# Packed half blocks in the second stage of a two-stage attention kernel, and two exponentials taken out of ScalarE's set order

## Chip, cores and metric

The kernel runs on one core of a Trainium2 chip. The metric is the device time of one execution in microseconds: the median of several runs. The profile is of one execution; its page's "span" goes from the first to the last instruction.

## What is computed

There are two stages. The first is attention with soft-capped scores over 8 batches, 12 heads, 448 positions, 64 per head. The second is a layer of four attention experts on its output (768 wide), causal, of which each position uses the two with the largest gate.

```python
# first stage
scores = scale * np.matmul(q, k.transpose(0, 1, 3, 2))
scores = cap * np.tanh(scores / cap)
attn = np.exp(scores - max); attn = attn / attn.sum(-1)
x = attn @ v                                   # then [batch, 448, 12 * 64]
# second stage
logits = x @ w_gate                            # 4 experts, the top 2 of each position kept
for e in range(4):
    q, k, v = x @ wq[e], x @ wk[e], x @ wv[e]  # 64 wide
    a = softmax(causal(scale * q @ k.T))
    ye = a @ v @ wo[e]
    out += (weight of e where e is chosen) * ye
```

## The kernel before

**First stage.** The 96 heads go in 48 pairs p (six pairs, `HP`, to a batch). A pair's scores are filled by TensorE into PSUM in three parts: "X" (two banks for a first chunk of 128 keys, a third for the last 64 keys of both heads), "Y1" and "Y2" (two banks each, one tile Y for both, so that Y2 can only be filled once ScalarE has read Y1). ScalarE takes the tanh of each part (`tanh`, L907) and then the exponential of a whole pair in one instruction (`expo`, L919). These instructions have a set order, `fixed=True`: X and Y1 of pair p, the exponential of pair p - 1, Y2 of pair p. The fills are `fill` and `heads` (L854) and `tails` (L864); the score matmuls of two heads sum over 64 rows each and sit in the two halves of TensorE's rows. The product with V is `pv` (L934, L942), its division `xk` on VectorE, its transposes `xt`. The pairs of the last batch (42 to 47) leave out their last queries, which come as two more units, 48 and 49 (`NPV` = 50).

**Second stage.** Batch b's work runs under the first stage's pairs of batch b + 1: V, gate and K and Q projections (`b_v`, `b_gate`, `b_qk`), then for each of two slots s (a position's first and second choice) a masked query qm, scores (`b_score`), one exponential, the causal masks (`causal`), the product with V (`b_pv`), then the sum of both slots (`b_ot`, on GpSimd, "POOL") and the output projection (`b_wo`). Since qm is zero where an expert isn't chosen, the four experts' scores are one matmul over 256 rows, done as two of 128 (r = 0, 1). From batch 4 on (`MD`) the mask is transposed by a DMA (mT). The scores of a slot are laid out in 1024 columns of two banks: three diagonal blocks of 128 by 128, and the rest below the diagonal, with two blocks of 64 columns at either end for the last 64 positions (`H0`, `H1`). The exponential (L1301) of the 1024 columns belongs to the set order: `exps` says after which pair's Y1 it stands; a pair in `alone` has its X fill apart from the fill of Y2 of the pair before. The mask is two selects on GpSimd (L1311, L1318). The product reads blocks of 128 by 128 from `cols(n)`: 1, 2, 3 and 4 matmuls of 260 columns for the four query blocks n.

**Batch 7** has no pairs after it: `last`, `last2` and `normed` do its second stage at the end, with its own layout (`eL` exponentials at L1577, masks at L1585) in the tiles pP of the other batches.

**Order of the work.** Every operation is entered in a graph with an engine, a planned duration (`occ`), what it reads and writes, and a due time. `dues` derives due times backwards from the set order of ScalarE (`when`); `solve` plays a list schedule and fixes the order in which each engine gets its instructions. `RANKS` holds, from a planned time on, offsets in hundredths of a microsecond to the due times of single operations. Engines run their queues in order; SyncE ("SP") issues most DMAs. PSUM banks are taken from `AUX` (three A banks), `XB` and `YB` by `Group`. The chip's waits follow from the tiles touched, not from the planned times; a row entered in the graph's write list only keeps the order.

Of the kernel before, what the change touches and what calls it, by code (L numbers as in the profile page):

```python
# [25 lines left out]
    (7.5, {  # L26
        136: 93, 174: 305, 290: -418,
    }),
    (27.5, {
        507: 475,  # L30
    }),
    (67.5, {
        678: -572, 692: 231, 735: -81, 738: -31, 741: 513, 841: 473, 1112: 748, 1167: -284,
    }),
    (87.5, {
        716: 497, 727: -643, 760: -112, 767: -1037, 862: 1282, 888: 375, 919: 264,
    }),
    (127.5, {
        1092: 467, 1196: 214, 1239: -453, 1249: 345, 1267: 323, 1277: 281, 1398: -60, 1401: 289,
        1405: 243, 1449: -132, 1535: 337, 1537: 820,  # L40
    }),
    (147.5, {
        1338: 97, 1345: 117, 1355: 477, 1387: -702, 1413: 186, 1525: 119, 1548: -196,
    }),
    (167.5, {
        1600: 205, 1607: 294,
    }),
# [7 lines left out]
    }),  # L55
    (254.5, {
        2520: -331, 2577: -265, 2635: -902, 2645: 2133, 2659: 128, 2667: 486, 2678: 522, 2702:
        -188, 2703: -340, 2706: -238, 2713: -937, 2729: -581, 2766: 2204, 2788: 297,
# [3 lines left out]
TURN = 2.2  # L62
SAIL = 1.1
SHIP = 1.25
# [10 lines left out]
MD = 4  # L75
# [23 lines left out]
class Graph:  # L99
# [232 lines left out]
def kernel(  # L332
# [26 lines left out]
    W1 = 320  # L359
# [90 lines left out]
    def turned(n, dst, src, r, w, name, due=None):  # L450
# [35 lines left out]
    pP = [sb(f"pP{i}", [128, 2, 64 + 1024]) for i in range(2)]  # L486
# [17 lines left out]
    vL = sb("vL", [128, E, Dh + 1])  # L504
    p2 = yp[NPV % NYP].rearrange("p a s -> p (a s)")[:, 0 : E * 512].rearrange(
        "p (e c t) -> p e c t", e=E, c=4)
    oTL = [sb(f"oTL{i}", [128, 2, 128]) for i in range(3)]
# [107 lines left out]
    def setup_b():  # L615
# [20 lines left out]

        def pz():
            for t in pB:
                nc.gpsimd.memset(t[:, 0:64], 0.0)

        gp(0.6, pz, w=[("pB", i) for i in range(4)])
# [110 lines left out]
    def tr(p):  # L752
# [45 lines left out]
        if p >= KD:  # L798
            pe(0, lambda: tq(g, 0, 2), [("q16", i), "ident"], [("tps", p, "q")], g, occ=0.1,
               name=f"trq{p}")  # L800
            pe(0, lambda: tq(g, 2, 4), [("q16", i), "ident"], [("tps", p, "r")], g, occ=0.1)
            def qe():
# [7 lines left out]
                [("qk", t, "q"), ("qkw", t)], g, name=f"qk{p}")  # L810
# [85 lines left out]
    alone = {0, 1, *exps}  # L896
# [228 lines left out]
    def b_v(b, ref):  # L1125
        x = b % 2
        j1 = PJ if b == LB - 1 else 0
        for n in range(4):
            g = Group(AUX + XB, 1.8)
            hr = [("half", "v", n)] if b == LB - 1 else []  # L1130
            for j0 in range(j1, NDC, 2):
# [14 lines left out]
                [("vps", b, n)] + hr, [("vB", x, n)], g, name=f"vB{b}")  # L1146

    def b_qk(b, ref):
        x = b % 2
        for r in range(2):  # L1150
            for which in "kq":
# [4 lines left out]
                for j in range(j1, NDC):  # L1156
# [4 lines left out]
                       [(which, b, r)], g, name=f"{which}{b}_{r}",  # L1161
# [81 lines left out]
    def b_mask(b, s):  # L1243
# [9 lines left out]
        if b < MD:  # L1253
            for r in range(2):
# [8 lines left out]
                pe(0, mm, [("mB", s), "ident"], [("mt", b, s, r)], g, occ=0.22, name=f"mT{b}")  # L1263
# [14 lines left out]
    def keys(c):  # L1278
        o = S - 128 if c == KC else 128 * c
        return slice(o, o + 128)  # L1280

    def b_score(b, s):
        x = b % 2
        for part, bk in ((H1, "X1"), (H0, "X0")):
            for i, (o, c, q0, n) in enumerate(part):
                def mm(o=o, c=c, q0=q0, n=n):
                    ps = BANK[f"X{o // 512}"]
                    a = min(n, max(KM - q0, 0))
                    for d, m, t in ((0, a, q0 + TL), (a, n - a, max(q0 - KM, 0))):
                        for r in range(2):  # L1290
                            if m:
                                nc.tensor.matmul(  # L1292
                                    ps[:, o % 512 + d : o % 512 + d + m], kB[x][r][:, keys(c)],
                                    qm[s][r][:, t : t + m], start=(r == 0), stop=(r == 1),
                                )

                pe(0, mm, [("kB", x, r) for r in range(2)] + [("qm", s, r) for r in range(2)],
                   [("s", bk)], occ=2 * c_pe(n), name=f"sB{b}_{s}", takes=(bk,) if i == 0 else ())
        pi = 2 * (b % 2) + s
        pb = pB[pi]  # L1300
        act(c_act(1024), lambda: nc.scalar.activation(  # L1301
            pb[:, 64:], PART["X"].rearrange("p a c -> p (a c)"), AF.Exp, scale=isc),
            [("s", "X0"), ("s", "X1")], [("pB", pi)], fixed=True, name=f"eB{b}_{s}",
            frees=("X0", "X1"))
        b_score.last = fixed_last()
        causal(pb, pi, "")

    def causal(pb, pi, nm):
        def diag():
            blk = pb[:, 128:512].rearrange("p (a c) -> p a c", a=3)  # L1310
            nc.gpsimd.affine_select(  # L1311
                out=blk, in_=blk, compare_op=ALU.is_ge, fill=0.0, base=0,
# [546 lines left out]
```

## Time and profile before

| | us |
|---|---|
| median of 3 runs | 305.21 (304.68 to 305.82) |
| the profiled execution | 304.79 |
| its span | 303.1 |
| ScalarE busy | 290.2 |
| TensorE busy (modelled ends) | 282.0 |
| VectorE busy | 213.5 |
| GpSimd busy | 189.4 |

The profiled execution's own time is 1.69 us longer than its span. A group of instructions in the profile reads: line, engine, operation, what is written and read, shapes, count, then busy time, mean ns of one, and the idle time of the engine just before. A row of a timeline reads: start, duration, then the instruction, with the idle time before it in brackets. A duration on ScalarE or TensorE overlaps the next instruction's, so that the cost of one is read from start to start.

### The profile page before, as it was taken

Reading aid. Unit: us, or ns where it says so; the run is one execution under the profiler, and the core shown is the slowest. Engines: PE = TensorE matmul, PEld = TensorE weight load, DVE = VectorE, ACT = ScalarE, POOL = GpSimd, SP = SyncE. Lnnn points to the kernel's source line nnn. Section 1 sums busy time; section 2 is a strip of 40 time slices with the busy share of each in tenths; the row PEclk is TensorE's granted clock in tenths of the full one; section 3 lists DMA queues with packets and bytes.
Section 4 is the critical chain, followed back from the end, with each engine's and each line's share of the span. In section 5 each row is a group of like instructions: output and inputs, shape, how many; then the busy total and the mean of one; then the engine's idle time right before and its main releaser. Section 6 shows DMA issues by size and latency. Waiting matters only on the chain.

```text
span 303.1 us, 8955 instructions
## 1 busy us (share of the span) xinstructions
PE 282.0 (93%) x3470; PEld 188.1 (62%) x3470; DVE 213.5 (70%) x630; ACT 290.2 (96%) x244; POOL 189.4 (62%) x537
## 2 busy tenths in 40 slices
PE   7897989999999999999999999999898999989992
PEld 4463546666666676667666676656665675657771
DVE  3354556866867877687887887697766878486972
ACT  5999999999999999999999999999999999989981
POOL 6793435997699664958799355927469305711580
PEclk9999999999999999999999999999999999999999
DMA  6999999999993399677996874455028751743136
GB/s 168 223 206 238 236 233 298 284 225 281 264 233 88 118 257 244 161 216 194 280 197 170 235 244 123 55 151 146 2 52 123 216 92 21 103 142 93 37 151 215
DMA packets 86874, 53.12 MB, mean 175 GB/s; under 512 B 47536, under 2 KB 83120, under 8 KB 86832
## 3 DMA queue, kind: packets, MB, share of 16 engines
q1 hardware_dynamic: 86448, 52.13, 69.8%
q8 instruction: 27, 0.44, 0.6%
q10 hardware_dynamic: 384, 0.43, 0.5%
q14 instruction: 15, 0.12, 0.2%
HBM read 36.19 MB, written 11.01 MB: 156 GB/s over the span
## 4 chain that ended last, share of the span: by engine, by line
ACT 64%; PE 15%; POOL 5%; DMA 5%; DVE 5%; issue 4%; ACTq 0%; DVEq 0%; POOLq 0%
ACT yp L907 33%; ACT yp L919 28%; ACT pP L1301 3%; DMA mT<-mB 3%; PE A L1413 2%; PE X L1292 2%; PE A L1088 2%; PE Y L854 1%; DMA ktf<-in_k_dram 1%; PE A L942 1%; POOL oS L1376 1%; POOL mB L1248 1%; PE A L1479 1%; DMA oT<-oS 1%; PE A L1514 1%
## 5 line engine op out<-in xcount | busy, mean ns | idle before, releaser
L919 ACT ACTIVATE yp<-yp 128x3136 f16<-128x3136 f16 (+4 forms) x51 | 142.4, 2794 | 0.0
L907 ACT ACTIVATE yp<-Y 128x896 f16<-128x896 f32 (+2 forms) x100 | 101.7, 1017 | 1.3 <-PE Y L854 1.3
L907 ACT ACTIVATE yp<-X 128x1344 f16<-128x1344 f32 (+2 forms) x50 | 68.3, 1367 | 0.4 <-PE X L854 0.3
L942 PE MATMUL A<-v,yp 128*128 128x65 f16 x1008 | 49.8, 193 | 0.0
L942 PEld LDWEIGHTS <-yp 128*128 128x128 f16 x1008 | 43.6, 97 | 4.0 <-issue 2.1
L934 PE MATMUL A<-vtz,yp 128*128 128x130 f16 x168 | 37.3, 222 | 3.9 <-ACT yp L919 1.6
L744 POOL CAST v<-vf 128x384 f16<-128x384 f32 x48 | 24.6, 519 | 20.8 <-PE A L942 13.1
L968 DVE TENSOR_TENSOR xk<-A,rca 128x256 f16<-128x256 f32 x84 | 35.3, 421 | 2.2
L708 POOL CAST q<-qf 112x512 f16<-112x512 f32 x44 | 26.6, 618 | 13.7 <-PE A L758 9.0
L439 DVE COPY ob<-A 128x384 f32<-128x384 f32 (+1 forms) x50 | 25.6, 550 | 2.4 <-PE A L1413 2.0
L817 DVE COPY qk<-A 128x960 f16<-128x960 f16 x32 | 20.3, 652 | 9.2 <-PE A L758 9.0
L934 PEld LDWEIGHTS <-yp 128*128 128x128 f16 x168 | 16.2, 97 | 16.1 <-issue 8.8
L854 PE MATMUL Y<-qk 64*128 64x448 f16 x136 | 24.7, 357 | 1.5 <-ACT yp L907 0.9
L1366 DVE SCALAR_TENSOR_TENSOR oB<-A,rcb,mw 128x256 f16<-128x256 f32 x55 | 25.3, 477 | 1.0
L1311 POOL TENSOR_SCALAR_AFFINE_SELECT pP<-pP 128x384 f16<-128x384 f16 x14 | 7.4, 528 | 29.3 <-ACT pP L1301 29.3
L965 DVE RECIPROCAL rca<-A 128x4 f32<-128x4 f32 x84 | 15.0, 178 | 14.2 <-PE A L942 13.2
L1413 PE MATMUL A<-wo,oT 128*128 128x384 f16 x106 | 22.8, 326 | 1.0 <-DVE qm L1170 1.0
L1351 PE MATMUL A<-vB,pP 128*128 128x260 f16 x138 | 22.2, 274 | 1.3 <-DVE oB L1366 0.5
L1028 DVE COPY xT<-A 128x448 f16<-128x448 f16 (+1 forms) x38 | 14.7, 386 | 11.2 <-PE A L1019 10.8
L1088 PE MATMUL A<-wvg,xT 128*128 128x260 f16 x168 | 21.3, 274 | 0.6 <-DVE oB L1366 0.3
L1376 POOL TENSOR_TENSOR oS<-oB,oB 128x512 f16<-128x512 f16 x14 | 16.1, 1155 | 8.2 <-issue 5.0
L758 PE MATMUL A<-ident,q 112*128 112x112 f16 x192 | 19.8, 214 | 0.7 <-DVE oB L1366 0.4
(240 smaller groups left out, 620.2 us busy)
## 6 DMA issues: line engine op xcount, KB each, us to landing
qf<-in_q_dram SPq DMA_DIRECT2D x23, 448.0 KB, 5.7
kf<-in_k_dram SPq DMA_DIRECT2D x23, 384.0 KB, 5.0
vf<-in_v_dram SPq DMA_DIRECT2D x23, 384.0 KB, 4.7
out_dram<-ob SPq DMA_DIRECT2D x21, 384.0 KB, 3.1
ktf<-in_k_dram SPq DMA_DIRECT2D x46, 32.0 KB, 5.0
vtf<-in_v_dram SPq DMA_DIRECT2D x46, 32.0 KB, 4.3
out_dram<-ob SPq DMA_DIRECT2D x6, 192.0 KB, 2.9
ob<-in_moe_wv_dram SPq DMA_DIRECT2D x2, 384.0 KB, 4.8
```

The source lines that it names most:

```text
L439: (nc.scalar.copy if o.eng == "ACT" else nc.vector.tensor_copy)(dst(), src())
L708: e(q16[i], qf[s][:, h].rearrange("p h (c d) -> p c h d", c=QC))
L744: nc.gpsimd.tensor_copy(v16[u][:, :, :, 0:Dh], vf[s][:, h].rearrange("p h (c d) -> p h c d", c=KC))
L854: nc.tensor.matmul(dst[:, g, o], kT[r, 128 * (c + 1) : 128 * (c + 2)], t[r, qs], start=True, stop=True,)
L907: ACTS[what, p] = act(c_act(n * (b - a)), lambda: nc.scalar.activation(y[:, a:b, 0:n], src[:, 0 : b - a, 0:n], AF.Tanh, scale=isc / capf), ...
L919: act(c_act(n * (b - a), False), lambda a=a, b=b, n=n: nc.scalar.activation(y[:, a:b, 0:n], y[:, a:b, 0:n], AF.Exp, scale=capf), ks, ks, f ...
L934: nc.tensor.matmul(ps[:, n, :, :], y[:, 2 * S + w : 2 * S + w + 128], vtz[u], start=(n == 0), stop=False, skip_group_check=True,)
L942: nc.tensor.matmul(ps[:, n, h, :], y[:, o : o + 128], v16[u][:, h, c, :], start=False, stop=(c == 2), skip_group_check=True,)
L968: dve(c_dve(128 * m), lambda g=g, i=i, rc=rc, m=m: nc.vector.tensor_tensor(xk[p % NXK][:, 2 * i : 2 * i + m, :, :], view(g)[:, 0:m, :, 0:D ...
L1088: nc.tensor.matmul(bank(g)[:, 0 : E * Dh + E], xT[x][:, j, WIN[n] : WIN[n] + 128], wvg[:, j, :], start=(j == j1), stop=(j == jn),)
L1366: dve(c_dve(E * Dh) + 0.06, lambda g=g, k_=k_, n=n: nc.vector.scalar_tensor_tensor(oB[s][:, n, :, :], view(g)[:, :, 0:Dh], rcb[k_][:, 0, : ...
L1413: nc.tensor.matmul(bank(g)[:, 0 : D // 2], oT[x][:, n // 2, r, n % 2, :], wo2[r][:, c0:c1], start=(r == 0), stop=(r == 1),)
```

## The change

The second stage's score layout shrinks from 1024 to 896 columns. Each of three diagonal blocks of 128 by 128 has an upper right quarter that the mask clears in full. Now the block's lower rows are stored with the columns below it (`ROWS`: 64 + 320, 64 + 192, 64 + 64 columns of full height), and the upper left quarters, 64 by 64, are stored two above one another (`HALF`), together with the last 64 positions' own block. A half block's score matmul has 64 output rows, in the lower or upper half of the PSUM tile. In the product a query block n takes the older keys as before, then its own half block (64 rows by 64 columns, output rows 0 to 63), then the 64 columns of full height (output rows 64 to 127). Block 1's half lies in partitions 64 to 127, so a copy of V's rows 0 to 63 of that block is made there by a DMA (vH, one for each batch). The masks become three selects of 128, 256 and 64 columns. The columns that held zeros, and their clearing (`pz`), go.

The exponentials of batch 6 are split in two of 448 columns each (`LOOSE`), take banks like any other work, and are no longer in the set order.

The rest: the products take only the A banks; batch 7's scores and outputs use other buffers (`pL`, `oBL`); some graph entries get one more write key, which orders a matmul behind an earlier reader of what its result will replace; set instructions planned after `START` have as due time their place in the set order alone; `TURN` is 3.0 for 2.2; `RANKS` is replaced (135 offsets).

```diff
+TURN = 3.0
+START = 15.0
+LOOSE = (0, 1)
...
-            o.due = d
+            o.due = when[o.idx] if when.get(o.idx, 0.0) > START else d
...
-    pP = [sb(f"pP{i}", [128, 2, 64 + 1024]) for i in range(2)]
+    pP = [sb(f"pP{i}", [128, 2, 896]) for i in range(2)]
...
+    pL = [free3[:, 2 * i : 2 * i + 2] for i in range(2)]
...
-    alone = {0, 1, *exps}
+    alone = {0, 1, *(p for p, (b, s) in exps.items() if b < LB - 1 or s not in LOOSE)}
...
+            if n == 1:
+                sp(lambda: nc.sync.dma_start(vH[x][64:128], vB[x][0:64, 1]), [("vB", x, 1)], [("vH", x)],
+                   name=f"vH{b}", lat=2.6)
...
-    H0 = ((0, KC, KM, 64), (64, 0, 0, 128), (192, 1, 128, 128), (320, 2, 256, 128),
-          (448, 2, KM, 64))
-    H1 = ((512, 0, 128, 320), (832, 1, 256, 192))
+    HALF = ((0, 0, 0, 0), (0, 64, KM, KM), (448, 0, 256, 256), (448, 64, 128, 128))
+    ROWS = ((64, 0, 64, 384), (512, 1, 192, 256), (768, 2, 320, 128))
...
+        gs = [Group(ANY, 1.5) for _ in range(2)] if b == LB - 1 and s in LOOSE else None
+        its = [[("r", *y) for y in ROWS if y[0] // 448 == i] + [
+            ("h", *y) for y in HALF if y[0] // 448 == i] for i in range(2)]
+        for i in (1, 0):
+            for m_, (kind, o, c, q0, n) in enumerate(its[i]):
+                lead = m_ == 0
+                if kind == "h":
+                    row, k0, q0, n = slice(c, c + 64), q0, n, 64
+                    kk = slice(k0, k0 + 64)
+                else:
+                    row, kk = slice(0, 128), slice(128 * c, 128 * (c + 1))
...
+                                    ps[:, d : d + m], kB[x][r][:, kk], qm[s][r][:, t : t + m],
+                                    start=(r == 0), stop=(r == 1), skip_group_check=True)
...
+            if gs:
+                act(c_act(448), lambda i=i, gs=gs: nc.scalar.activation(
+                    pb[:, 448 * i : 448 * (i + 1)], bank(gs[i])[:, 0:448], AF.Exp, scale=isc),
+                    [("sf", b, s, i)], [("pB", pi)], gs[i], name=f"eF{b}_{s}")
+        if not gs:
+            act(c_act(896), lambda: nc.scalar.activation(
+                pb.rearrange("p (a c) -> p a c", a=2), PART["X"][:, 0:2, 0:448], AF.Exp, scale=isc),
+                [("s", bk[0]), ("s", bk[1])], [("pB", pi)], fixed=True, name=f"eB{b}_{s}",
+                frees=bk[0:2])
...
+        gp(0.28, lambda: keep(two[0:64, :, 0:64], [0, 2], [1, 64]), [], [("pB", pi)], name="diag")
+        gp(0.42, lambda: keep(two[64:128, :, 0:128].rearrange("p a (b c) -> p a b c", b=2),
+                              [0, 2], [0, 2], [1, 64]), [], [("pB", pi)], name="diag")
+        gp(0.2, lambda: keep(pb[64:128, 768:832], [1, 64]), [], [("pB", pi)], name="diagt")
...
-            g = Group(AUX + XB, 1.6)
+            g = Group(AUX, 1.6)
+            its = []
+            for c in range(min(n, KC)):
+                o = ROWS[c][0] + WIN[n] - ROWS[c][2]
+                its.append((slice(0, 128), slice(o, o + 128), slice(0, 128), vB[x][:, c]))
+            if n < KC:
+                p0, o = own(n)
+                v_ = vH[x] if n == 1 else vB[x][:, n]
+                its.append((slice(p0, p0 + 64), slice(o, o + 64), lo64, v_))
+                o = ROWS[n][0]
+                its.append((slice(0, 128), slice(o, o + 64), hi64, vB[x][:, n]))
+            else:
+                its.append((hi64, lo64, hi64, vB[x][:, n]))
...
+                        nc.tensor.matmul(
+                            bank(g)[q_, 0 : E * (Dh + 1)], pb[rows, cs], v_[rows],
+                            start=(t == 0 or len(its) == 2), stop=(t >= len(its) - 2),
+                            skip_group_check=True)
```

More of the change, by code (lines that the diff above doesn't have):

```diff
@@ L1160, in b_qk @@
                                (f"w{which}2", 2 * r), (f"w{which}2", 2 * r + 1)],
-                       [(which, b, r)], g, name=f"{which}{b}_{r}",
+                       [(which, b, r)] + ([("qm", s, r) for s in range(2)]
+                                          if which == "q" and b >= MD else []), g, name=f"{which}{b}_{r}",
                        due=(ref, 25.225 + 9.62 * r + 13.055 * (which == "q")))
@@ L1299, in b_score @@
[L1299 to L1305, printed above, removed]
+                   [("sf", b, s, i) if gs else ("s", bk[i])], gs and gs[i], occ=2 * c_pe(n),
+                   name=f"sB{b}_{s}", takes=(bk[i],) if lead and not gs else ())
@@ new lines, in b_score @@
+            if gs:
[7 more added lines that the diff above has]
+                frees=bk[0:2])
+            b_score.last = fixed_last()
@@ L1323, in causal, with keep @@
-        gp(0.6, diag, [], [("pB", pi)], name="diag")
-        gp(0.25, tail, [], [("pB", pi)], name="diagt")
-    def cols(n):
-        res = []
-        for c in range(min(n, KC - 1) + 1):
-            if c == n:
-                o = 64 + H0[1 + c][0]
-            elif c == 2:
-                o = 64 + H0[3][0] + 64
-            else:
-                o = 64 + H1[c][0] + WIN[n] - 128 * (c + 1)
-            res.append((c, o))
-        if n == 3:
-            res.append((3, 0))
-        return res
+        def keep(blk, *pat):
+            nc.gpsimd.affine_select(out=blk, in_=blk, compare_op=ALU.is_ge, fill=0.0, base=0,
+                                    pattern=list(pat), channel_multiplier=-1)
@@ L1577, in scores @@
                 act(c_act(W1), lambda e=e, pi=pi, o=o: nc.scalar.activation(
[L1578 to L1580 removed]
+                    pL[r][:, e, o : o + W1], bank(g2[e])[:, 0:W1], AF.Exp, scale=isc),
+                    ["pLfree", k0 if e == 0 else ("sL", r, part, 2)],
+                    [("pL", pi, part)], g2[e],
                     name=f"eL{part}{pi}")
@@ L1587, in below @@
                         pattern=[[0, 2], [1, 128]], channel_multiplier=-1)
-                gp(0.38, below, [], [("pB", pi, part) for pi in (2 * r, 2 * r + 1)], name="diagL")
+                gp(0.38, below, [], [("pL", pi, part) for pi in (2 * r, 2 * r + 1)], name="diagL")
+        pe(0, lambda: None, [], ["pLfree"] + [("yp", (PB + 5) % NYP, w) for w in SL], occ=0.0,
+           name="op")
         for part in range(2):
```

135 lines of the change are left out of this document (65 added, 70 removed), and 23 rows, old and new, of the table RANKS.

## The prediction

> **What bounds the kernel now.** I read the page first: the busy shares and the chain that ended last.
>
> ```profile
> span 303.1 us, 8955 instructions
> ...
> PE 282.0 (93%) x3470; PEld 188.1 (62%) x3470; DVE 213.5 (70%) x630; ACT 290.2 (96%) x244; POOL 189.4 (62%) x537
> ...
> ACT 64%; PE 15%; POOL 5%; DMA 5%; DVE 5%; issue 4%; ACTq 0%; DVEq 0%; POOLq 0%
> ```
>
> ScalarE (ACT) is busy nearly throughout and carries the chain; TensorE (PE) stands close behind. Next the chain in order of time, in a stretch with one second-stage exponential (L1301):
>
> ```profile
> 61.04 2.71 ACT yp L919
> 63.75 2.79 ACT yp L907 x3
> 66.54 2.71 ACT yp L919
> 69.25 0.92 ACT pP L1301
> 70.16 2.79 ACT yp L907 x3
> 72.96 2.71 ACT yp L919
> ```
>
> One period (a head pair's three tanhs and one long exponential) is 66.54 - 61.04 = 5.50 us; with a second-stage exponential it is 72.96 - 66.54 = 6.42. Nothing lies between: ScalarE sets the pace. Its own timeline (start, duration) gives what one instruction costs, from start to next start:
>
> ```profile
> 68.91 1.26 ACT L1301 ACTIVATE pP<-X 128x1024 f16<-128x1024 f32 x1
> 69.81 1.16 ACT L907 ACTIVATE yp<-Y 128x896 f16<-128x896 f32 x1
> 70.62 1.53 ACT L907 ACTIVATE yp<-X 128x1344 f16<-128x1344 f32 x1
> 71.80 1.15 ACT L907 ACTIVATE yp<-Y 128x896 f16<-128x896 f32 x1
> 72.60 3.06 ACT L919 ACTIVATE yp<-yp 128x3136 f16<-128x3136 f16 x1
> ```
>
> 1024 columns cost 0.90 us, 896 cost 0.80 (71.80 to 72.60), 1344 cost 1.18; so 448 columns are 0.38 us and an instruction of 448 is some 0.80 - 0.38 = 0.42.
>
> ScalarE's largest holes outside the start stand at batch 6's first second-stage exponential:
>
> ```profile
> 267.43 1.02 ACT L1301 ACTIVATE pP<-X 128x1024 f16<-128x1024 f32 x1 [0.85 <-PE X L1292]
> ...
> 269.38 0.97 ACT L907 ACTIVATE yp<-X 128x960 f16<-128x960 f32 x1 [0.33 <-PE X L854]
> ...
> 260.37 5.33 DMA mT<-mB
> ...
> 265.73 0.64 DVE qm L1170
> ```
>
> A transpose by DMA takes 5.33 us, qm is late, the scores are late, and ScalarE waits 0.85 + 0.33 = 1.18 us in its fixed order.
>
> How full is TensorE really? Its busy time is modelled, so I take its pace from starts:
>
> ```profile
> 137.14 0.49 PE L1413 MATMUL A<-wo,oT 128*128 128x384 f16 x2
> 137.46 0.61 PE L1292 MATMUL X<-qm,kB 128*128 128x64 f16 x10
> ...
> 139.99 0.36 PE L854 MATMUL X<-qk 64*128 64x448 f16 x2
> 140.28 0.23 PE L934 MATMUL A<-vtz,yp 128*128 128x130 f16 x1
> 140.35 0.35 PE L942 MATMUL A<-v,yp 128*128 128x65 f16 x6
> 140.53 0.33 PE L1019 MATMUL A<-perm,xk 128*128 128x128 f16 x3
> 140.70 0.22 PE L1019 MATMUL A<-pswap,xk 128*128 128x128 f16 x1
> 140.85 0.36 PE L854 MATMUL Y<-qk 64*128 64x448 f16 x2
> ```
>
> Two matmuls of 384 columns take 0.32 us: 0.417 ns a column. Six of 65 take 0.18 where 390 x 0.417 = 0.16: some 2.5 ns more for each. The pair of 64-row matmuls of L854 runs side by side, 448 x 0.417 = 0.19 us for both, yet the next work starts 0.29 after it: leaving the 64-row shape costs 0.10. Entering it costs the same: the four transposes at 140.53 are 512 columns, 0.21 us, and the pair starts 0.32 after them. I use 0.097 a change of shape. Before has 240 such changes in its instruction order, all between 128 and 64 rows.
>
> **The change, part by part.** *Packing on ScalarE.* Twelve exponentials (batches 0 to 5) shrink from 1024 to 896 columns: 12 x 0.10 = -1.2 us, on the path, where nothing covers ScalarE. *Batch 6 loose.* Two of 1024 become four of 448: 4 x 0.42 - 2 x 0.90 = -0.12. They stand outside the set order now, the first two after pair 47's tanhs instead of before pair 46's last, so the 5.33 us transpose no longer holds the tanhs: -1.18. What is late next is batch 6's own output:
>
> ```profile
> 277.94 0.85 ACT L907 ACTIVATE yp<-Y 128x768 f16<-128x768 f32 x1
> ...
> 280.49 2.45 ACT L919 ACTIVATE yp<-yp 128x2688 f16<-128x2688 f16 x1
> ...
> 285.94 0.45 ACT L1577 ACTIVATE pP<-Y0s 128x320 f16<-128x320 f32 x1
> ```
>
> Its last exponential ended 285.94 - 277.94 = 8.0 us before the set order's end; now its last stands right ahead of the 280.49 one, 5.4 us before. Sum on ScalarE: -2.5 us.
>
> *Packing on TensorE.* Each batch and slot gets 13 products with V for 10, and 20 score matmuls for 18: 14 x 5 = 70 more, 3540 in all. The 42 products of 260 columns are 42 x 0.108 = 4.5 us; scores lose a little. The larger item is shape. Half blocks have a 64-column output (scores: 128 rows by 64 columns; products: 64 by 64, then 128 by 64), so each n of the product goes through two or three shapes. The new order has 405 changes: 224 between row shapes (16 fewer, as batch 6 no longer parts fills) and 181 into, out of or among 64-column shapes. No trace here has a 64-column shape. Bounds: nothing, or as the nearest row, 0.097: 181 x 0.097 = 17.6 us of TensorE time. I take 0.097: a shape that differs in columns is set up like one that differs in rows, and the row is the only price there is.
>
> The Trainium skill, "TensorEngine Tiling (Array Packing)", Key Properties, says that a change of tiling mode, not merely of tile, drains the engine. The trace agrees for rows, 0.10 us each; it has none for columns. By the rule the sum stays as with 0.097.
>
> What of this reaches the path? I count TensorE's need from one pair's first Y fill to the next pair's, in the new order, beside ScalarE's period (5.50, or 6.42 - 0.10 = 6.32 with an exponential; counted at 6.30). TensorE works in order and the Y fill may not start before the last tanh of Y, so work of a period cannot run ahead. Pair 12: 12532 columns (side-by-side partners once) x 0.417 = 5.22, 88 matmuls x 0.0025 = 0.22, 15 changes x 0.097 = 1.46: 6.90, over by 0.60. Pair 24: 5.07 + 0.25 + 14 x 0.097 = 6.68, over by 0.38; before it was 5.80 of 6.42. Counted alike, twelve periods go over: 12 by 0.60, 14 by 0.27, 17 by 0.26, 18 by 0.23, 19 by 0.28, 24 by 0.38, 25 by 0.05, 26 by 0.52, 29 by 0.08, 31 by 0.32, 36 by 0.21, 38 by 0.12: 3.3 us. In before none does; the fullest was 6.03 of 6.42. A full period also has no room for TensorE's waits on banks and copies; I add 0.1 for each of the twelve, 1.2 (bounds 0 and 0.2 each). At no cost for column shapes, only pair 17 goes over, by 0.07.
>
> *The end.* From pair 42's first Y fill on, the need rises from 46.2 to 50.9 us, 43 of the column changes being there.
>
> ```profile
> 266.00:286.00 20.00, 19.34 (x248) 13.53 (x248) 16.51 (x50) 18.82 (x19) 4.68 (x10) 1.00 0.31 92
> ```
>
> TensorE (first number after the length) is full from 266 to 286, where batch 6's products now fall; behind that the end waits on gates and copies more than on it. I put 0.7 of the 4.7 on the path; bounds 0 and 4.7.
>
> *Edits at nothing.*
>
> ```profile
> L1351 PE MATMUL A<-vB,pP x138: 271/274/285, 74.2 to 283.3; 128*128 128x260 f16 x138
> ...
> L1311 POOL TENSOR_SCALAR_AFFINE_SELECT pP<-pP x14: 522/527/535, 70.2 to 278.2; 128x384 f16<-128x384 f16 x14
> L1318 POOL TENSOR_SCALAR_AFFINE_SELECT pP<-pP x14: 237/238/240, 70.8 to 278.8; 64x64 f16<-64x64 f16 x14
> ...
> L1585 POOL TENSOR_SCALAR_AFFINE_SELECT pP<-pP x6: 407/410/416, 287.3 to 290.9; 128x256 f16<-128x256 f16 x6
> ...
> ktf<-in_k_dram SPq DMA_DIRECT2D x46, 32.0 KB, 5.0
> ...
> 234.21 0.53 SPq L1427 DMA_DIRECT2D out_dram<-ob  x1
> ...
> L907 ACT ACTIVATE yp<-Y 128x896 f16<-128x896 f32 (+2 forms) x100 | 101.7, 1017 | 1.3 <-PE Y L854 1.3
> ...
> L942 PEld LDWEIGHTS <-yp 128*128 128x128 f16 x1008 | 43.6, 97 | 4.0 <-issue 2.1
> ```
>
> The masks become three selects of 128, 256 and 64 columns: between 0.238 and 0.410 by length, 0.30 + 0.41 + 0.24 = 0.95 for 0.77, so 0.18 later. The first product starts 74.2 - 71.0 = 3.2 us after the masks; that covers it, else it is 0.18 x 14. The seven vH copies (33 KB; nearest row 32 KB, 5.0 us) take some 0.53 of SyncE's queue each, ahead of loads and transposes, and their readers come about five periods, 27 us, later (four shorter ones in batch 6); uncovered, a product and everything behind it on TensorE would wait up to 5 us. Products in three banks instead of six, other buffers for the last batch's scores and outputs, new loading order at the start, due times: 0, and together within 1.3 either way, the longest wait of a tanh in before, at the start (L907's row).
>
> *Sum.* -2.5 + 3.3 + 1.2 + 0.7 = +2.7. The profiled execution took 304.79, its span 303.1 plus 1.69 around it: 307.5. The median, 305.21, is 0.42 above it, which gives 307.9; I say 307.8.
>
> **The rivals.** *Column shapes cost nothing* (0.32, the other side). Place: the half blocks; price: 0 a change; it decides once a change is under about 0.03 us, for then 12 periods hold their excess. For it: columns of one array share their rows' stream, and no row shows a loss. Against: the 0.10 of all row changes. Time: 305.21 - 2.5 = 302.7.
>
> *Changes cost, but are taken up* (0.05). Fills of Y2 have 2.7 us of cover by the long exponential, and the planner may have left room in lighter periods such as 15 and 16 (4.9 and 4.5 of 5.50). Against it: the Y fill of every period is a barrier. Half the excess, nothing at the end: 305.21 - 2.5 + 1.7 = 304.4.
>
> *Worse: column weights load slowly too* (0.08). Weight loads take 97 ns (L942's row), hidden today under starts 30 ns apart. If 210 loads of 64-column weights came into the open by a fifth of that, +4 us of TensorE, most of it in full periods: 311.
>
> The Trainium skill, "TensorEngine Tiling (Array Packing)", Tile-to-Partition Mapping (Restrictions), says that column tiling switches Fast Weight Load off. No run here shows it.
>
> **How the numbers follow.** My forecast has 0.55 and its own range 305.6 (no extra room lost, end unhurt) to 311 (0.2 a full period, half of 4.7 at the end). Half a percent, 1.5 us, is about what a measurement of this kernel tells from no change: faster means below 303.7, slower above 306.7. Slower: 0.46 of the forecast's 0.55 and the worse rival's 0.08, 0.54. Same: 0.08 of the forecast, 0.04 of the taken-up case, 0.01 of the free one, 0.13. Faster: 0.31 of the free case and crumbs, 0.33. The range takes in the free case: 302.0 to 311.0.
>
> **What would show it.** Right: TensorE starts after a 64-column shape 0.1 late, ScalarE holes of 0.2 to 0.6 us released by Y or X fills in pairs 12, 18, 24, 26, 31, and no hole at batch 6. The packed exponential at 0.80 shows the gain. Wrong: matmuls of 64 columns following full ones without a gap; then ScalarE's chain ends some 2.5 us earlier and the time is near 302.7. Also wrong: a hole ended by vH, or an end longer than 17 us after the last set exponential.

## The result and the profile after

| | before | after |
|---|---|---|
| median, us | 305.07 (304.68 to 305.82) | 313.85 (313.66 to 314.03) |
| ratio, 95% interval | | 1.0285 (1.0263 to 1.0307): slower |
| profiled execution / its span | 304.79 / 303.1 | 314.03 / 312.3 |

The change costs 8.8 us, where 2.6 were forecast; the medians here are of four executions each. First the page of the changed kernel: the span, the busy time of the engines, the shares of the chain that ended last, and from its list of groups ScalarE's two groups of tanhs (busy, mean, idle time in front and what ended it).

```profile
span 312.3 us, 9116 instructions
...
PE 295.4 (95%) x3540; PEld 188.1 (60%) x3540; DVE 217.9 (70%) x629; ACT 291.5 (93%) x247; POOL 191.3 (61%) x547
...
PE 71%; ACT 17%; DVE 5%; POOL 3%; DMA 1%; issue 1%; ACTq 0%; POOLq 0%; DVEq 0%
...
L930 ACT ACTIVATE yp<-Y 128x896 f16<-128x896 f32 (+2 forms) x100 | 93.1, 931 | 4.1 <-PE Y L877 3.8
L930 ACT ACTIVATE yp<-X 128x1344 f16<-128x1344 f32 (+2 forms) x50 | 64.4, 1289 | 3.5 <-PE X L877 3.5
```

The chain has changed hands: ScalarE had 64% of it, now TensorE has 71%. TensorE's modelled busy time rose by 13.4 us with 70 short matmuls more, and the tanhs, which stood 1.7 us idle before, stand 7.6, nearly all of it for the fills of Y and X. So ScalarE is no longer fed.

Where this arises is read in one place, pair 36, the second of two exponentials of a batch. ScalarE's timeline after (start, duration, idle time in brackets):

```profile
217.15 2.82 ACT L942 ACTIVATE yp<-yp 128x3136 f16<-128x3136 f16 x1
219.86 0.92 ACT L1341 ACTIVATE pP<-X 128x896 f16<-128x896 f32 x1
220.66 0.93 ACT L930 ACTIVATE yp<-Y 128x896 f16<-128x896 f32 x1
222.52 1.29 ACT L930 ACTIVATE yp<-X 128x1344 f16<-128x1344 f32 x1 [0.94 <-PE X L877]
```

The packed exponential costs 220.66 - 219.86 = 0.80, as worked out. The next tanh starts 222.52 - 220.66 = 1.86 later, 1.06 more than its 0.80; 0.94 of that the row shows as idle, until X is filled. TensorE's timeline after, in the same stretch:

```profile
215.75 0.36 PE L877 MATMUL Y<-qk,kd 64*128 64x448 f16 x2
...
218.06 0.36 PE L887 MATMUL X<-qk,kd 128*128 128x448 f16 x1
218.26 0.27 PE L1387 MATMUL A<-vB,pP 128*128 128x260 f16 x1
218.46 0.29 PE L1387 MATMUL A<-vH,pP 64*64 64x260 f16 x1
218.69 1.53 PE L1387 MATMUL A<-vB,pP 128*64 128x260 f16 x7
220.16 0.36 PE L877 MATMUL Y<-qk,kd 64*128 64x448 f16 x2
220.45 0.77 PE L781 MATMUL A<-ident,q 112*128 112x112 f16 x8
221.26 0.22 PE L957 MATMUL A<-vtz,yp 128*128 128x130 f16 x1
...
222.12 0.36 PE L877 MATMUL X<-qk,kd 64*128 64x448 f16 x2
...
222.96 0.36 PE L877 MATMUL Y<-qk,kd 64*128 64x448 f16 x2
```

260 columns stream in 0.11 us, yet the 64 by 64 product starts 0.20 after the full one, the 128 by 64 product 0.23 after that. From the first product to the Y fill pass 1.90 us for nine products, without a gap that another engine causes. The X fill follows 1.96 later, and it is this fill that the tanh waits for. In these 1.96 us TensorE itself stands: eight transposes of 112 columns, 8 x 112 x 0.417 = 0.37 us of streaming, take 221.26 - 220.45 = 0.81. In this stretch the chain goes over VectorE, which reads the products' output out of its banks:

```profile
220.43 0.39 DVE oB L1402
```

The first and the last row are the first Y fills of two pairs: this period took TensorE 222.96 - 215.75 = 7.21 us, beside 6.30 of ScalarE. The same nine products in full shape are shown with the first experiment.

The end grew too. ScalarE after, from the last set exponentials on:

```profile
289.61 2.53 ACT L942 ACTIVATE yp<-yp 128x1920 f16<-128x1920 f16 x2
294.70 0.44 ACT L1613 ACTIVATE yp<-X2s 128x320 f16<-128x320 f32 x1 [2.56 <-PE X2s L1603]
...
298.07 0.21 ACT L1676 ACTIVATE gt<-gt 128x12 f32<-128x12 f32 x1 [1.43 <-POOL gt L1675]
```

I split every run here: the set order ends where the row of the last two set exponentials ends, the rest of the span is the end. After: 289.61 + 2.53 = 292.14, and 312.3 - 292.14 = 20.2. Before: 283.51 + 2.54 = 286.05, and 17.05. Of the 9.2 us more of span, 6.1 lie in the set order and 3.1 in the end, which now begins with 2.56 us of waiting for batch 7's first scores and has 1.43 more for its gate; before, ScalarE went into these scores without a wait. What stands in front of the scores is shown by the stretch from 266 to 292, engine by engine (length, then PE, PEld, DVE, ACT, POOL, clock, DMA share, GB/s), TensorE being full for all of it:

```profile
266.00:292.00 26.00, 26.00 (x308) 16.42 (x307) 18.37 (x47) 25.47 (x26) 8.68 (x22) 1.00 0.39 101
```

### The profile page after: what moved, and what is told of

Read it like the earlier page. It is cut to its first block, busy times and chain, and to the rows that moved or that the text cites. A ratio compares the mean times of both kernels' runs of the same rounds, so it can differ in the third digit from the quotient of the medians.

```text
span 312.3 us, 9116 instructions
## 1 busy us (share of the span) xinstructions
PE 295.4 (95%) x3540; PEld 188.1 (60%) x3540; DVE 217.9 (70%) x629; ACT 291.5 (93%) x247; POOL 191.3 (61%) x547
## 4 chain that ended last, share of the span: by engine, by line
PE 71%; ACT 17%; DVE 5%; POOL 3%; DMA 1%; issue 1%; ACTq 0%; POOLq 0%; DVEq 0%
PE A L1387 11%; PE A L1119 10%; ACT yp L930 9%; ACT yp L942 8%; PE A L965 8%; PE Y L877 7%; PE A L1111 5%; PE A L1449 5%; PE A L957 4%; PE X L1329 4%; PE X L887 3%; PE X L877 3%; PE A L1042 3%; PE A L781 2%; PE A L791 2%; DVE kB L1106 1%
## 5 line engine op out<-in xcount | busy, mean ns | idle before, releaser
L942 ACT ACTIVATE yp<-yp 128x3136 f16<-128x3136 f16 (+4 forms) x51 | 138.0, 2707 | 0.0
L930 ACT ACTIVATE yp<-Y 128x896 f16<-128x896 f32 (+2 forms) x100 | 93.1, 931 | 4.1 <-PE Y L877 3.8
L930 ACT ACTIVATE yp<-X 128x1344 f16<-128x1344 f32 (+2 forms) x50 | 64.4, 1289 | 3.5 <-PE X L877 3.5
L1387 PE MATMUL A<-vB,pP 128*128 128x260 f16 (+2 forms) x168 | 36.0, 286 | 0.1
L988 DVE RECIPROCAL rca<-A 128x4 f32<-128x4 f32 x84 | 15.1, 179 | 20.2 <-PE A L965 19.0
L1350 POOL TENSOR_SCALAR_AFFINE_SELECT pP<-pP 64x128 f16<-64x128 f16 (+2 forms) x42 | 12.7, 318 | 26.8 <-ACT pP L1337 12.8
L1387 PEld LDWEIGHTS <-pP 128*128 128x128 f16 (+2 forms) x182 | 16.8, 101 | 19.8 <-issue 10.7
L1402 DVE SCALAR_TENSOR_TENSOR oB<-A,rcb,mw 128x256 f16<-128x256 f32 x56 | 26.1, 479 | 1.4
L716 POOL CAST k<-kf 128x384 f16<-128x384 f32 x33 | 16.3, 509 | 15.0 <-PE A L791 7.2
L1111 PE MATMUL A<-wvg,xT 128*128 128x260 f16 x168 | 22.1, 274 | 0.1
L1449 PE MATMUL A<-wo,oT 128*128 128x384 f16 x100 | 21.7, 327 | 0.1
```

Source lines behind the costliest of these rows:

```text
L930: ACTS[what, p] = act(c_act(n * (b - a)), lambda: nc.scalar.activation(y[:, a:b, 0:n], src[:, 0 : b - a, 0:n], AF.Tanh, scale=isc / capf), ...
L942: act(c_act(n * (b - a), False), lambda a=a, b=b, n=n: nc.scalar.activation(y[:, a:b, 0:n], y[:, a:b, 0:n], AF.Exp, scale=capf), ks, ks, f ...
L1111: nc.tensor.matmul(bank(g)[:, 0 : E * Dh + E], xT[x][:, j, WIN[n] : WIN[n] + 128], wvg[:, j, :], start=(j == j1), stop=(j == jn),)
L1387: nc.tensor.matmul(bank(g)[q_, 0 : E * (Dh + 1)], pb[rows, cs], v_[rows], start=(t == 0 or len(its) == 2), stop=(t >= len(its) - 2), skip_ ...
L1402: dve(c_dve(E * Dh) + 0.06, lambda g=g, k_=k_, n=n: nc.vector.scalar_tensor_tensor(oB[s][:, n, :, :], view(g)[:, :, 0:Dh], rcb[k_][:, 0, : ...
L1449: nc.tensor.matmul(bank(g)[:, 0 : D // 2], oT[x][:, n // 2, r, n % 2, :], wo2[r][:, c0:c1], start=(r == 0), stop=(r == 1),)
```

## The experiments

The theory after the result: a column change costs a row change's 0.1 us, and it is lost nearly in full where products stand in front of a fill, period by period, since a fill has less room there than my count over a whole period allows. Rivals: the order, the banks or the vH copies cost; every change costs the same share wherever it stands; the loose exponentials spoil the end. A further rival, that the sums of the periods were too low to begin with, has no run of its own; the rows of pair 36 bear on it.

In x1, x2, x3, x7 and x12 to x15, matmuls of full shape stand in place of half blocks, with the same operands' neighbours in them, so that the half blocks' part of the second stage is overwritten or wrong; in x9 the first 64 output rows of two of its three products lack their last block of keys. Nothing else is left out.

**x1: all half blocks in full shape.** The order of the instructions stays that of after; rows 0 to 63 of vH, which the full shape reads too, are cleared at the start.

```diff
-row, k0, q0, n = slice(c, c + 64), q0, n, 64
-kk = slice(k0, k0 + 64)
+k0, n = min(q0, S - 128), 64
+row, kk = slice(0, 128), slice(k0, k0 + 128)
...
 rows, cs, q_, v_ = its[t]
+o_ = min(cs.start, 896 - 128)
+rows, cs, q_ = slice(0, 128), slice(o_, o_ + 128), slice(0, 128)
```

> The changed kernel with the same order, the same 3540 matmuls and the same columns, but every half-block score and every product of the second stage issued as a full 128 by 128 shape (the quarter that a 64-column shape would leave alone is computed too, so the second stage's output differs). 181 changes into, out of or among 64-column shapes go, 10 row changes come back. Theory (the shape changes cost 0.10 to 0.12 us each and overfill TensorE's periods): TensorE needs some 19 us less, the holes of ScalarE in the periods with products go, the set order ends some 7 us earlier, the end shrinks by about 3: 302 to 305 us. Rival (the new order, the three banks for the products, the copies vH or the new start make the loss): at most 2 us better than the changed kernel's 313.9, so 311 or more.

Measured: 303.21 us, ratio 0.9946 (0.9914 to 0.9978). Without column changes the whole loss is gone; order, banks, copies and masks are as in after, and those rivals fall. TensorE's timeline of x1, same place:

```profile
211.64 0.35 PE L888 MATMUL X<-qk,kd 128*128 128x448 f16 x1
211.83 0.27 PE L1390 MATMUL A<-vB,pP 128*128 128x260 f16 x1
211.94 0.27 PE L1390 MATMUL A<-vH,pP 128*128 128x260 f16 x1
212.05 0.94 PE L1390 MATMUL A<-vB,pP 128*128 128x260 f16 x7
212.93 0.36 PE L878 MATMUL Y<-qk,kd 64*128 64x448 f16 x2
...
214.90 0.36 PE L878 MATMUL X<-qk,kd 64*128 64x448 f16 x2
```

and ScalarE's tanh of that X in x1:

```profile
215.37 1.43 ACT L931 ACTIVATE yp<-X 128x1344 f16<-128x1344 f32 x1
```

The nine products take 212.93 - 211.83 = 1.10 us where after took 1.90: 0.80 for seven changes more. From the Y fill to the X fill pass 1.97 where after took 1.96: the wait for VectorE is in both. The tanh starts at 215.37 with no wait, but the fill's record ends at 214.90 + 0.36 = 215.26: it had 0.1 us of room. Two more stretches of this period grew, read from their rows' starts to the next row's: the 20 scores just ahead, 1.02 us after and 0.90 in x1, and the four products ahead of them, 0.66 and 0.46. So 0.80 + 0.12 + 0.20 = 1.12 us, less the 0.1 of room, give 1.0 of the 1.06 by which the tanh is late.

**x2 and x3: one half of x1 each**, the scores alone, the products alone, in full shape.

> The changed kernel with only the half-block score matmuls issued as full 128 by 128 shapes (second stage's output differs); the products keep theirs. 145 of 181 column changes stay, of which the costlier ones from 64 by 64 to 128 by 64 (0.117 us). Theory: the scores carry 36 of 181 changes and get about a fifth of the loss back: 311 to 313 us. Rival (order or banks): 313.9, no change.

> The changed kernel with only the products issued as full 128 by 128 shapes (second stage's output differs); the half-block scores keep their 64-column shape. 36 of 181 column changes stay. Theory: four fifths of the loss go: 304 to 307 us. Rival (order or banks): 311 or more.

Measured: x2 312.2 us (1.0212, 1.0149 to 1.0275, two executions), x3 304.34 (0.9959, 0.9934 to 0.9984). As expected: the products' shapes carry 9.5 of the 10.6 us between after and x1, the scores' 1.1 to 1.7.

**x14 and x15: column shapes in some batches only.** x14 keeps them in batches 0 to 2 (74 changes), x15 in batches 3 to 6 (107).

```diff
+if b < 3:
     row, k0, q0, n = slice(c, c + 64), q0, n, 64
     kk = slice(k0, k0 + 64)
+else:
+    k0, n = min(q0, S - 128), 64
+    row, kk = slice(0, 128), slice(k0, k0 + 128)
...
+if not (b < 3):
+    o_ = min(cs.start, 896 - 128)
+    rows, cs, q_ = slice(0, 128), slice(o_, o_ + 128), slice(0, 128)
```

> The kernel after with the 64-column shapes in batches 0 to 2 alone; from batch 3 on the half blocks are full 128 by 128 as in x1. 74 of the 181 column changes stay. Theory (each period loses for itself what it is over full, and more than I counted): the loss is what ScalarE stood in the profile of after in pairs 12 to 26, 0.81 + 0.47 + 0.26 + 0.82 + 0.24 + 0.31 + 0.53 + 0.48 + 0.82 = 4.7 us, less some 0.9 that x1 stands in the same pairs: 3.8 above x1's 303.2, 306.5 to 307.5. Rival (a backlog of TensorE grows through the whole run and is paid late): half of the changes costs far less than half, 304 to 305.5.

> The other half: 64-column shapes in batches 3 to 6, 107 of the 181 changes. Theory (each period for itself): the two halves add up, 313.85 - 303.2 = 10.6 us less the 3.8 of batches 0 to 2: 6.8 above x1, 309.4 to 310.5. Rival (a backlog through the whole run): 306.5 to 308.5.

Measured: x14 307.09 us (1.0082, 1.0060 to 1.0105), x15 309.78 (1.0165, 1.0146 to 1.0184). Above x1 that is 3.9 and 6.6, together 10.5 of 10.6: the losses add, each period for itself, and no backlog grows. ScalarE in x14 and then in x15, the last set exponentials and the first of batch 7:

```profile
284.07 2.74 ACT L943 ACTIVATE yp<-yp 128x1920 f16<-128x1920 f16 x2
287.51 0.44 ACT L1621 ACTIVATE yp<-X2s 128x320 f16<-128x320 f32 x1 [0.69 <-PE X2s L1611]
```

```profile
285.56 2.53 ACT L943 ACTIVATE yp<-yp 128x1920 f16<-128x1920 f16 x2
290.65 0.44 ACT L1621 ACTIVATE yp<-X2s 128x320 f16<-128x320 f32 x1 [2.56 <-PE X2s L1611]
```

The set order ends at 286.81 and 288.09. The wait of 2.56 us at the end is there only where batch 6 has column shapes; its part above x14's 0.69 is 1.9.

**x8 and x9: column changes without the change.** The kernel before, in which the last product of a query block writes output rows 64 to 127 only: in x8 for block 3 (28 changes), in x9 for blocks 1 to 3 (84), which is the one shown.

```diff
+h_ = 64 if t == len(cs) - 1 and len(cs) > 1 else 0
-bank(g)[:, 0 : E * (Dh + 1)], pB[pi][:, o : o + 128],
+bank(g)[h_:128, 0 : E * (Dh + 1)], pB[pi][:, o + h_ : o + 128],
```

> The kernel before, complete, in the same order, with one matmul of each slot's products (the last 64 positions' own block) issued with 64 output columns instead of 128, whose other half was zeros: 28 column changes more, no column of work more. Theory (overfull periods): in before only pair 14's period goes over, by 0.13 us; 305.1 to 306 us. Rival (each change costs 0.065 us): 305.1 + 1.8, 306.7 to 307.2 us.

> The kernel before in the same order, with the last matmul of three of each slot's four product groups issued with 64 output columns (for two of them half of its output rows are left out, so the output differs): 84 column changes more, no work more. Counted with 0.105 us a change, the excess over ScalarE's periods is 0.31 us, and eleven periods come within 0.3 of full. Theory (overfull periods): 305.5 to 307.5 us, part of it at the end. Rival (each change costs 0.065 us): 305.1 + 5.5, 310 to 311 us.

Measured: x8 305.36 us (1.0011, 0.9988 to 1.0034), x9 307.2 (1.0079, 1.0050 to 1.0107). Per change x9 loses 2.4 / 84 = 0.03 us, x14 0.053, x15 0.062, and x8 nothing that can be told. One price for every change does not fit; a loss that depends on the room where a change stands does.

**x5: one column shape for all.** V copies padded with zeros (vZ, written by GpSimd) let both short products of a block be 128 by 64, next to one another in the order; 118 changes stay.

```diff
-p0, o = own(n)
-v_ = vH[x] if n == 1 else vB[x][:, n]
-its.append((slice(p0, p0 + 64), slice(o, o + 64), lo64, v_))
+v_ = vH[x] if n == 1 else vZ[x][:, n // 2]
+both = [(slice(0, 128), slice(o, o + 64), lo64, v_)]
...
+both.append((slice(0, 128), slice(o, o + 64), hi64, vB[x][:, n]))
```

> The changed kernel, complete, with the products' half blocks brought into one shape: the own half block is multiplied over all 128 rows by V rows padded with zeros, so that it and its partner are both 128 rows by 64 columns, side by side in the two column halves; the half blocks of query block 1 and of the last 64 positions swap places, and the latter's product is a full 128 by 128. Column changes fall from 181 to 118, and the two 260-column products of a pair overlap. Counted as in the prediction with 0.105 us a change, the excess of TensorE's need over ScalarE's periods falls from 4.0 us to 0.4. Theory (time is lost where a period is overfull): 303.5 to 306 us. Rival (each column change costs its own 0.065 us of the total, as 9.5 us for 145 changes in the run with full products suggests): 63 changes fewer, 309 to 310.5 us.

Measured: 305.46 us (1.0029, 1.0001 to 1.0057), everything computed. 63 changes fewer than after give back 8.4 us. TensorE in x5:

```profile
214.06 0.30 PE L1394 MATMUL A<-vH,pP 128*64 128x260 f16 x1
214.06 0.52 PE L1394 MATMUL A<-vB,pP 128*64 128x260 f16 x2
```

Two products in the two column halves start together; with equal shapes the halves run side by side, which is a second part of the gain.

**x4: the planner is told the price**, 0.1 for a score half, 0.1 to 0.33 for a group of products.

```diff
-occ=2 * c_pe(n),
+occ=2 * c_pe(n) + 0.1 * (kind == "h"),
```

> The changed kernel, complete, with the planner told what the shapes cost: 0.1 us more for each half-block score, and 0.1 to 0.33 more for each product's step with 64-column shapes; offsets kept. Column changes stay (187). Theory (TensorE's need itself overfills the periods): the order moves, little is gained, 310 to 313 us. Rival (the need would fit, the changes only came unplanned, so that fills were late): most of the loss goes, 307 or less.

Measured: 324.23 us (1.0604, 1.0561 to 1.0647), a miss for both. Its list of groups has the wait moved to the second-stage exponentials, its timeline the loose ones behind the set order:

```profile
L1342 ACT ACTIVATE pP<-X 128x896 f16<-128x896 f32 x12 | 11.9, 991 | 8.5 <-PE X L1329 6.7 <-POOL v L767 1.8
```

```profile
288.03 2.62 ACT L942 ACTIVATE yp<-yp 128x1920 f16<-128x1920 f16 x2
291.87 0.54 ACT L1338 ACTIVATE pP<-X1s 128x448 f16<-128x448 f32 x1 [1.22 <-DVE qm L1197]
```

The 135 offsets belong to one order. With other costs another order comes out, and the end takes 322.7 - 290.65 = 32.1 us. What a planner with its offsets found anew would reach was not tried.

**x7, x12, x13: the longer end.** x1's end is 18.2 us for 17.05 before. Its rows on ScalarE:

```profile
280.06 2.73 ACT L943 ACTIVATE yp<-yp 128x1920 f16<-128x1920 f16 x2
283.48 0.44 ACT L1616 ACTIVATE yp<-X2s 128x320 f16<-128x320 f32 x1 [0.70 <-PE X2s L1606]
...
286.84 0.21 ACT L1679 ACTIVATE gt<-gt 128x12 f32<-128x12 f32 x1 [1.42 <-POOL gt L1678]
```

x7 is x1 with batch 6's exponentials back in the set order (`LOOSE = ()`). x12 plans the subtraction in front of the gate's exponential earlier on GpSimd and that exponential one place later; x13 moves both further.

```diff
-lat=occ + 0.13, name="g3")
+lat=occ + 0.13 + (0.9 if w_ == "z" and r_ == "lm" and tag == 3 else 0),
+name="g3z" if w_ == "z" and r_ == "lm" and tag == 3 else "g3")
...
+if u.name == "g3z":
+    d -= 6.0
```

> The run with full shapes everywhere (no column changes, second stage's output differs), but with batch 6's two exponentials back in ScalarE's set order as one instruction each; offsets stay with the same operations. Theory A (the loose exponentials are what takes away the hole of 1.2 to 1.6 us at batch 6, and what makes the end after the set order 1.4 us longer, since batch 6's products come later): the set order ends about 1.5 us later, the end is about 1.4 shorter, time 302.7 to 304 us against 303.2. Rival B (the longer end has another cause: due times, buffers): 304.3 to 305.5 us.

> This is x1 (full shapes, no column changes) with the gate's exponential of the last batch one place later on ScalarE and its subtraction two operations earlier on GpSimd. In x1 the end behind the last set exponential is 18.56 us for 17.14 before, and ScalarE stands 1.42 us for that exponential. Theory: this wait is what lengthened the end. Then the two operations, 0.34 and 0.28 us, and the one place, 0.42 us, come off the wait, and the time is 303.2 - 0.6 to -1.0: 302.2 to 302.6. Rival: the end is set by TensorE's copies and products behind it and the wait is cover: 302.9 to 303.6, as x1.

> This is x1 with the gate's subtraction ahead of all masks of the last batch on GpSimd, as it nearly is in before, and its exponential behind three more exponentials on ScalarE. Theory (the wait for the gate lengthened the end by 1.4 us): the 1.42 us wait is gone, the end is 17.1 to 17.5 us, the time 301.8 to 302.3. Rival (the end is set by TensorE, the wait is cover): 302.9 to 303.6.

Measured: x7 304.8 us (0.9995, 0.9969 to 1.0021), x12 303.72 (0.9964, 0.9942 to 0.9985), x13 304.47 (1.0002, 0.9978 to 1.0026). Both theories fell. x7 came out as its rival said: taking the exponentials out of the set order gains some 1.6 us and doesn't spoil the end. x12 and x13 gained nothing and lie above their rivals' 303.6 too; in x12 the gate's exponential no longer waits, so this wait was not what set the end. The chain of x1, in order of time, tells why; below it the chain of x12:

```profile
284.65 0.42 POOL yp L1624
285.07 0.23 POOL g_c L1681
...
293.17 0.20 POOL g_k L1691
...
294.46 0.23 DVE slL L1487
```

```profile
284.36 4.33 DMA oT<-oS
288.75 0.29 POOL oTL L1511
289.04 0.36 POOL yp L1626
```

In x1 the end hangs on GpSimd's queue of masks and gate steps, one after another from 284.65 to 293.37, behind a first mask that waits for batch 7's first exponential; VectorE's weights (slL) and the last projections follow on it. In x12 the shift brought a copy that waits for a transpose (4.33 us) ahead of the masks. Of the 1.2 us by which x1's end is longer than before's, some 0.8 lies in front of batch 7's first exponential, which waits 0.70 us for its scores in x1 and not at all in before. From this exponential on x1 takes 301.0 - 283.48 = 17.52 us and before 303.1 - 285.94 = 17.16: the other 0.4, where GpSimd carries the chain. No run removed either.

**x16: a complete kernel with few changes.** x5 with the half blocks behind the columns below them and 64 columns of zeros beside them in SBUF, so that blocks 0, 1 and 3 have products of 128 by 128 only; 64 changes stay. x17 also puts the score halves of both banks behind one another (60 changes).

```diff
-pP = [sb(f"pP{i}", [128, 2, 896]) for i in range(2)]
+pP = [sb(f"pP{i}", [128, 2, 1024]) for i in range(2)]
...
-HALF = ((0, 0, 0, 0), (0, 64, 128, 128), (448, 0, 256, 256), (448, 64, KM, KM))
-ROWS = ((64, 0, 64, 384), (512, 1, 192, 256), (768, 2, 320, 128))
+HALF = ((384, 0, 0, 0), (384, 64, 128, 128), (832, 0, 256, 256), (832, 64, KM, KM))
+ROWS = ((0, 0, 64, 384), (448, 1, 192, 256), (704, 2, 320, 128))
...
-its.append((slice(0, 128), slice(384, 512), slice(0, 128), vB[x][:, n]))
+its.append((slice(896, 1024), every, vB[x][:, n]))
```

> A complete kernel, nothing left out: the half blocks lie behind the columns below them, 64 columns of zeros stand beside them in SBUF, and the products of query blocks 0, 1 and 3 are all 128 by 128 (block 2's own two stay 128 by 64, side by side); scores as in after. 64 of the 181 column changes stay, ScalarE's 896 columns and the loose exponentials too; the mask is four selects, and GpSimd copies a part of V with zeros. Theory (the loss is the changes in front of the fills): some 304.0 to 305.0, within 1 us of x3's 304.34, where the products were full shapes but left the half blocks' result out. Rival (x1 and x3 were fast because of what they left out, the packing itself costs): 307 or more.

> As x16, with the two score halves of both banks behind one another, 60 column changes. Theory: no more than 0.5 us from x16, since those few changes stand where the period has room: 304.0 to 305.2. Rival: 307 or more.

Measured: x16 304.97 us (1.0013, 0.9996 to 1.0029), x17 312.26 (1.0242, 1.0211 to 1.0273). x16 does all of after's work 8.9 us faster, so the loss was the shapes and not what x1 left out. It is no faster than before; no complete kernel here is. Its groups of tanhs stand 1.5 us idle for after's 7.6:

```profile
L938 ACT ACTIVATE yp<-Y 128x896 f16<-128x896 f32 (+2 forms) x100 | 96.3, 963 | 0.9 <-PE Y L885 0.9
L938 ACT ACTIVATE yp<-X 128x1344 f16<-128x1344 f32 (+2 forms) x50 | 65.7, 1315 | 0.6 <-PE X L885 0.5
```

x17 is a miss for both: the graph entry that chains the halves gave another order, as in x4, with its second pair of loose exponentials behind the set order and an end of some 25 us. It says nothing of the changes.

## Why the prediction was wrong

The direction and the mechanism were right: column shapes cost what row shapes cost, and the loss is ScalarE waiting for fills. The terms for the periods (4.5 us for 8.0) and for the end (0.7 for 3.1) were too small. The measured column adds up ScalarE's starts, pair by pair, less what the instructions cost where nothing waits; the end is the split above.

| term | forecast | after less before |
|---|---|---|
| ScalarE's shorter and split exponentials | -1.3 | -1.4 |
| the hole at batch 6, and other waits from pair 42 on | -1.2 | -0.5 |
| the twelve periods counted as overfull | +3.3 + 1.2 | +5.5 |
| all other periods up to pair 41 | 0 | +2.5 |
| the end | +0.7 | +3.1 |
| sum | +2.7 | +9.2 |

**The price of a change.** I took 0.097 for shapes that no trace showed. The starts above give 0.20 - 0.11 = 0.09 into the 64 by 64 shape and 0.23 - 0.11 = 0.12 from it to 128 by 64. The rival in which columns cost nothing fell. The Trainium skill, "TensorEngine Tiling (Array Packing)", Key Properties, has a change of tiling mode drain the engine; the trace now agrees for columns too, with these numbers.

**"I add 0.1 for each of the twelve."** This is the step that failed first, together with the count that it is added to. The excess of a period over ScalarE's was the right place to look: the twelve periods hold 5.5 us. But the sums were too low. Pair 36 was counted at 6.30 + 0.21 = 6.51 us, and 0.1 for waits; TensorE took 7.21. Of the 0.70 between them, 0.4 is the wait for VectorE that the rows above show, and 0.3 is work and changes counted too cheaply. That period is 0.91 over ScalarE's 6.30, and ScalarE lost 1.06; only the last 0.15 is a matter of place, the fill having 0.1 us of room with the changes ahead of it. In pairs 14, 26 and 31 the starts show no wait of TensorE, and still it took 6.00, 6.30 and 6.13 from one pair's first Y fill to the next, counted at 5.77, 6.02 and 5.82. The price of a change alone does not explain that: at 0.105 the same count has 4.0 us of excess (the expectation of x5), for 3.3. Periods that I had counted as not over full lost 2.7 us (pairs 20, 23, 30, 32, 35, 40; before loses 0.8 in three of them), and these the count left out. How much of the loss in the other pairs is the sum and how much the place of the changes was not read one by one, and no run separates the two.

The count could have been tried on the trace of before. It has no period over full there, yet by ScalarE's starts before loses 0.3, 0.3 and 0.4 us in pairs 17, 35 and 40.

**"I put 0.7 of the 4.7 on the path."** Measured 3.1, an end of 20.2 us; one longer than 17 was named as a sign of being wrong, though before's own has 17.05. Some 2.7 of the 3.1 is TensorE's: full up to 292, it delivers batch 7's first scores 2.56 us behind the end of the set order, in before 0.1 ahead of it. Of this 1.9 goes when batch 6 has no column shapes (a wait of 0.69 in x14). I had read TensorE as full to 286 and assumed that later work waits on gates and copies more than on it; but the masks start behind those scores. The rest, some 0.4, lies behind the scores and is in x1 as well.

**What held.** The packed exponential at 0.80; the holes in pairs 12, 18, 24, 26 and 31 (0.81, 0.82, 0.48, 0.82, 0.40), against 0.2 to 0.6 forecast. The hole in front of batch 6's first second-stage exponential is gone, as this timeline row of after shows, which has no idle time; but at 285.27 a tanh now stands 0.48 us for a fill of Y, and by the table 0.5 of the 1.2 was gained:

```profile
277.98 0.98 ACT L1337 ACTIVATE pP<-A 128x448 f16<-128x448 f32 x2
```

The edits at nothing: the vH copies land in time, as the view of that tile after has it, and nobody waited for them.

```profile
L1387 PE MATMUL A<-vH,pP x14: 295/295/295, 73.7 to 290.0; 64*64 64x260 f16 x14
...
DMA to landing us min/median/max: 1.7/1.8/4.7
```

**The worse rival**, slow weights of 64 columns, fell as a mechanism of its own. Weight loads of after by shape (busy, mean ns):

```profile
L1387 PEld LDWEIGHTS <-pP 128*128 128x128 f16 x84 | 6.9, 97 | 3.9 <-issue 1.9
...
L1387 PEld LDWEIGHTS <-pP 128*64 128x64 f16 x42 | 4.5, 106 | 5.1
```

106 ns for 97 is a few per cent of what was lost, so the loads are hardly slower; what comes into the open is a load at each change, as the last section shows. Its 311 was nearer the time than my forecast, for another reason.

## What to carry to other kernels

Where an in-order engine feeds a bound one through fixed points, take the length of its periods from a trace, with the waits that are in them, and not from a sum of columns and changes: pair 36 ran 7.21 us where the sum had 6.51. Then price an addition at the next feeding point behind it: its whole length less the room that this point has, read from the trace as the time between the end of a fill and the start of its reader. In pair 36 that gives 1.0 of 1.06 us. Test such a count first on the kernel before. A layout that saves columns on one engine by giving another new shapes is to be laid out so that equal shapes stand together (x5), or padded to the full shape with zeros (x16). And a hand-fitted order may not survive a change of the costs or dependences that it was fitted with: x4 and x17 took 324.23 and 312.26 us.

## What was not expected of the hardware

The trace points to what a change of shape waits for. Weight loads after, and then in x1 (start, duration of the row):

```profile
218.07 0.10 PEld L1387 LDWEIGHTS <-pP 128*128 128x128 f16 x1
218.46 1.02 PEld L1387 LDWEIGHTS <-pP 64*64 64x64 f16 x6 [0.29 <-issue]
```

```profile
211.64 1.07 PEld L1390 LDWEIGHTS <-pP 128*128 128x128 f16 x9
```

A full product's weights are loaded while the matmul in front still streams: at 218.07 for a product that starts at 218.26, and in x1 from 211.64 on for products from 211.83 on. The load of the 64 by 64 shape starts at 218.46, with its own product and 0.20 after the one in front. So in this stretch a change of shape lays one weight load open, and the excess of 0.09 to 0.12 is about as long as such a load (0.10). That this is all of the price was not tested by itself.
